# DeltaNet and a cosine-gated layer on one core: the key scales worked out in unused columns of a PSUM bank

## The chip, the cores and the metric

The kernel runs on one core of one Trainium2 chip. The metric is the time of one execution in microseconds on the device; the median of several executions is given. TensorE (PE in the profile, PEld its weight loads) multiplies matrices, VectorE (DVE) and ScalarE (ACT) work element by element, GpSimd (POOL) does so too, and SyncE (SP) issues most DMA transfers. SBUF is the working memory; PSUM takes the results of TensorE and can also be read and written by VectorE and ScalarE.

## The reference

Two layers, one after the other. Batch 4, 8 heads, 768 steps, head size 48:

```python
k_n = k / (np.linalg.norm(k, axis=-1, keepdims=True) + 1e-06)
for t in range(S):
    kt, vt, bt = (k_n[:, :, t], v[:, :, t], beta[:, :, t, None])
    y[:, :, t] = np.einsum('bhd,bhde->bhe', q[:, :, t], state)
    v_old = np.einsum('bhde,bhd->bhe', state, kt)
    state = state + bt[:, :, :, None] * np.einsum('bhd,bhe->bhde', kt, vt - v_old)
...
h = x @ w_in
g = h * np.cos(h)
return (g @ w_out).astype(np.float32)
```

Here x is y with its heads side by side: 3072 rows of 384. w_in has 2048 columns, and w_out leads back to 384. The norm of each key, with 1e-6 added, divides the key. The kernel keeps the keys as they are and moves the norm into two factors: beta / norm squared, which it multiplies into small tiles, and the norm itself, which it multiplies into the values v.

## The kernel before

The 768 steps are cut into 24 units of 32 steps. For each unit the kernel transposes keys and queries, forms the products of keys with keys and with queries (`gram`, L652), inverts a triangular matrix, and carries the state on: `through_state` (L907), `right_side` (L924), `solve` (L979), `solve_out` (L991), `update` (L1004), `update_out` (L1012, the state's addition on VectorE), `within` (L1034), `features` (L1055). Units 0 and 1 are inverted by doubling on TensorE (L736, L749 to L756), the others row by row on GpSimd (L856, L863; for units 2 and 3 partly on VectorE), with trips through DRAM. Units 2 and 3 have a further half step (`solve_half` L937, `between_out` L957, `solve` L973).

Every two units give 256 rows for the second layer, a "p". Its first products go to the three banks `p_h` (L1076 for the first two p, then L1250 by a scheme with fewer multiplications that needs sums of inputs and of weights); ScalarE and VectorE make g of them (L1113, L1120, L1129, L1132, with helpers L1262, L1264, L1267, L1348). The products with w_out go to the bank `p_out` (L1274 for the first p, then L1332 in seven products of 16 matmuls in the trace, written as two halves), from which ScalarE (L1371) and VectorE (L1384) collect them.

`p_out` is a tile of 2 x 256 fp32 columns, 2 KB for each partition. The products use 192 columns of either half in turn (`place`), `output` the first 384, and `keep_warm` (L492) writes the first 256 with products that nobody reads, until the first output begins; it fills TensorE in start-up. Columns 448 to 511 are used by nothing.

The scales of the keys come from a chain of small operations for each pair m of units: ScalarE squares the keys (L554), VectorE sums them over the head (L559), GpSimd raises the sum to the power 0.5 (L571, tile `knrm`), and then `scale` on VectorE adds 1e-6 (L582, in place), squares (L584), takes the reciprocal (L585), and forms `bs` = beta times it (L587) and `bz`, the same once for each of two kinds of row, masked by the constant `odd` (L590). For the first two pairs each unit has a call of its own with 8 columns; after them one call does both units with 16 columns. That makes 14 calls. `bs` and `bz` are read by `gram_keys` (L664, L673) and `solve_out`. `weigh` (L607) multiplies the values by the norm, in the later pairs after a copy that exchanges halves (L603, L605).

The order of all work is written out by hand: `Order.add` (L207) takes each task with its dependencies, and `Order.run` emits them in the sequence of the long string `LINE` (L101); every engine is then pinned to that order. So each engine executes its tasks in the written order, and an instruction that waits holds all behind it on its engine. The waits themselves are derived from which instructions read and write which tiles; they aren't written out in the kernel.

Of the kernel before, what the change touches and what calls it, by code (L numbers as in the profile page):

```python
# [10 lines left out]
FP = mybir.dt.float32  # L11
I32 = mybir.dt.int32
U32 = mybir.dt.uint32
ALU = mybir.AluOpType
# [225 lines left out]
def kernel(  # L240
# [32 lines left out]
    nc = tc.nc  # L273

    B, H, S, D = q.shape
# [17 lines left out]
    const = ctx.enter_context(tc.tile_pool(name="const", bufs=1))  # L293
# [3 lines left out]
    work = ctx.enter_context(tc.tile_pool(name="work", bufs=2))  # L297
# [27 lines left out]
    def half(i):  # L325
        return slice(DP * i, DP * i + DP)
# [105 lines left out]
    odd = consts[:, 128 + C : 130 + C]  # L432
# [9 lines left out]
    for b in range(B):  # L442
        nc.gpsimd.dma_start(
            out=bq[C * b : C * b + H].rearrange("p n t -> p (n t)"), in_=beta[b]
# [2 lines left out]

    halves = const.tile([128, 2, H], FP, name="halves")
    nc.vector.memset(halves, 0.5)
    tiny = const.tile([128, 2, H], FP, name="tiny")  # L450
    nc.vector.memset(tiny, 1e-6)
    halfpi = const.tile([128, 1], FP, name="halfpi")
    nc.vector.memset(halfpi, math.pi / 2.0)

# [9 lines left out]
    bt = const.tile([128, NU, H], FP, name="bt")  # L464
# [18 lines left out]

    HM = DM // 2
    p_out = psum.tile([128, 2, 256], FP, name="p_out", tag="o", bufs=1)


    out_begun = []
# [89 lines left out]
    def scale(m, part):  # L578

        n = part.stop - part.start  # L580
        bs, bz, knrm = (t[:, part] for t in scales[m])
        nc.vector.tensor_tensor(out=knrm, in0=knrm, in1=tiny[:, 0:n], op=ALU.add)  # L582
        krec = work.tile([128, 2, H], FP, name="krec")[:, 0:n]
        nc.vector.tensor_tensor(out=krec, in0=knrm, in1=knrm, op=ALU.mult)  # L584
        nc.vector.reciprocal(krec, krec)  # L585
        first = 2 * m + part.start
        nc.vector.tensor_tensor(  # L587
            out=bs, in0=bt[:, first : first + n], in1=krec, op=ALU.mult
        )
        nc.vector.tensor_tensor(  # L590
            out=bz,
            in0=bs[:, :, :, None].to_broadcast([128, n, H, 2]),
            in1=odd[:, None, None, :].to_broadcast([128, n, H, 2]),
            op=ALU.mult,
        )

    def weigh(m):

        vp, knrm = vps[m], scales[m][2]
        if 2 * m >= PLAIN_TURNS:  # L600

            t = work.tile([128, 2, H], FP, name="krec")
            nc.vector.tensor_copy(t[:, :, 0::2], knrm[:, :, 0::2])  # L603
            for i in range(2):
                nc.vector.tensor_copy(t[half(i), :, 1::2], knrm[half(1 - i), :, 1::2])  # L605
            knrm = t
        nc.vector.tensor_tensor(  # L607
            out=vp,
            in0=vp,
            in1=knrm[:, :, :, None].to_broadcast([128, 2, H, D]),  # L610
            op=ALU.mult,
        )

    def turn(n, tag):
# [346 lines left out]
    first, spare = {}, {}  # L961
# [431 lines left out]
    def store(p, i, cols=slice(0, DM)):  # L1393
# [7 lines left out]
        for b in range(B):  # L1401
# [9 lines left out]
            x=2, x_sum=XS, turns=2, g=GATES, o=2, o_out=2,  # L1411
# [59 lines left out]
    def unit(n):  # L1471
# [20 lines left out]
        if n < 4 or not second:  # L1492
            add(("square", m, a), "ACT", 0.2 + 0.37 * width, lambda: norms_square(m, part),
                [("k", 2 * m + x) for x in range(part.start, part.stop)],
                makes=[("g", ("ksq", m, a))])
            add(("sum", m, a), "DVE", 0.2 + 0.4 * width, lambda: norms_sum(m, part),
                [("square", m, a)], makes=[("ksum", ("ksum", m, a))], uses=[("ksq", m, a)])
            add(("norms", m, a), "POOL", 0.4 + 1.28 * width, lambda: norms_root(m, part),
                [("sum", m, a)] + ([("norms", m, 0)] if a else []),
                makes=[] if a else [("scales", ("scales", m))], uses=[("ksum", m, a)])  # L1500
            add(("scale", m, a), "DVE", 1.1, lambda: scale(m, part),
                [("norms", m, a), ("beta",) if n < PLAIN_TURNS else ("beta_home",)])
        scaled = ("scale", m, a if n < 4 else 0)
        if second:
            add(("weigh", m), "DVE", 1.1 if n < PLAIN_TURNS else 1.5, lambda: weigh(m),
                [("v", n - 1), ("v", n), ("scale", m, 0), scaled])
# [419 lines left out]
```

## Time and profile before

| what | value |
|---|---|
| time, median of 3 runs (lowest, highest) | 639.16 us (639.09, 640.67) |
| the profiled execution's own time | 643.63 us |
| its span, from the first to the last instruction | 641.8 us |
| TensorE busy up to 110 us, and from 110 to 642 us | 95.06 us, 525.93 us |
| VectorE busy in the same two stretches | 73.51 us, 422.26 us |
| granted TensorE clock in the same | 0.95, 1.00 |
| L582, VectorE, 14 instructions, start of the first and the last | 11.7 us, 451.4 us |

How to read it: a line such as `L582 DVE TENSOR_TENSOR knrm<-knrm,tiny` names the line of the kernel, the engine, the operation, and the tile written and those read. In the timeline the first number is the start in us from the span's start, the second the duration of the row, `x2` the number of instructions in it, and square brackets hold the idle time of that engine ahead of it and what ended it. A TensorE instruction on fp32 data shows as two rows in the trace, but for the transposes.

### The profile page before, as it was taken

Reading aid. Unit: us, or ns where it says so; the run is one execution under the profiler, and the core shown is the slowest. Engines: PE = TensorE matmul, PEld = TensorE weight load, DVE = VectorE, ACT = ScalarE, POOL = GpSimd, SP = SyncE. Lnnn points to the kernel's source line nnn. Section 1 sums busy time; section 2 is a strip of 40 time slices with the busy share of each in tenths; the row PEclk is TensorE's granted clock in tenths of the full one; section 3 lists DMA queues with packets and bytes.
Section 4 is the critical chain, followed back from the end, with each engine's and each line's share of the span. In section 5 each row is a group of like instructions: output and inputs, shape, how many; then the busy total and the mean of one; then the engine's idle time right before and its main releaser. Section 6 shows DMA issues by size and latency. Waiting matters only on the chain.

```text
span 641.8 us, 24181 instructions
## 1 busy us (share of the span) xinstructions
PE 621.0 (97%) x10176; PEld 577.7 (90%) x10176; DVE 495.8 (77%) x1025; ACT 297.6 (46%) x528; POOL 435.2 (68%) x780
## 2 busy tenths in 40 slices
PE   5999989999999999999999999999999999999997
PEld 4867877997899999999999999999999999999997
DVE  5786746788899999887888898888888786656682
ACT  3447645563334454643642544643643553545440
POOL 5337787778778788888789887886883883112231
PEclk9899989999999999999999999999999999999999
DMA  9869565563551454435436235243304102000000
GB/s 186 213 141 236 103 163 121 117 119 54 101 81 22 92 91 70 88 69 83 79 64 103 49 68 101 51 65 66 72 4 82 41 2 42 19 2 26 1 25 25
DMA packets 209380, 50.36 MB, mean 78 GB/s; under 512 B 200920, under 2 KB 204280, under 8 KB 209272
## 3 DMA queue, kind: packets, MB, share of 16 engines
q1 hardware_dynamic: 161896, 35.03, 29.2%
q10 hardware_dynamic: 47072, 13.25, 9.9%
q8 instruction: 80, 1.31, 0.8%
q0 software_dynamic: 304, 0.54, 0.4%
q14 instruction: 28, 0.23, 0.1%
HBM read 38.55 MB, written 10.22 MB: 76 GB/s over the span
## 4 chain that ended last, share of the span: by engine, by line
PE 88%; DVE 5%; DMA 3%; issue 1%; ACT 1%; SPq 0%; POOL 0%; ACTq 0%; DVEq 0%
PE p_out L1332 28%; PE p_h L1250 27%; PE p_h L1076 7%; PE p_kq L907 4%; PE p_out L1274 3%; PE p_s L1004 3%; PE p_g L652 3%; PE p_kq L1034 3%; PE p_u L979 2%; PE p_h L736 2%; PE p_out L492 2%; PE p_h L1332 2%; PE p_z L1055 1%; DMA kp<-in_k_dram 1%; DMA out_dram<-o 1%
## 5 line engine op out<-in xcount | busy, mean ns | idle before, releaser
L856 POOL TENSOR_TENSOR part<-z,gb 128x126 f32<-128x126 f32 (+23 forms) x321 | 142.5, 444 | 42.8 <-DMA gb<-g_dr 13.7
L863 POOL TENSOR_TENSOR z<-z,part 128x126 f32<-128x126 f32 (+23 forms) x321 | 146.0, 455 | 25.2
L1332 PE MATMUL p_out<-w_out,g_ffn 128*128 128x192 f32 x672 | 121.8, 328 | 1.3 <-ACT o L1371 0.7
L1332 PEld LDWEIGHTS p_out<-w_out,g_ffn 128*128 128x128 f32 x672 | 107.7, 190 | 2.5 <-ACT o L1371 0.8
L1129 ACT ACTIVATE turns<-turns,halfpi 128x512 f32<-128x512 f32 x96 | 68.0, 719 | 55.7 <-DVE turns L1120 43.0
L1332 PE MATMUL p_out<-w_sum,g_ffn 128*128 128x192 f32 x496 | 89.7, 329 | 0.2 <-DVE o L1384 0.2
L1250 PE MATMUL p_h<-x_sum,w_in 128*128 128x128 f32 x640 | 84.0, 277 | 0.0
L1332 PEld LDWEIGHTS p_out<-w_sum,g_ffn 128*128 128x128 f32 x496 | 79.6, 190 | 1.2 <-issue 0.4
L1113 ACT ACTIVATE turns<-g_ffn,quarter_turn 128x512 int32<-128x512 f32 x70 | 49.8, 719 | 66.1 <-DVE g_ffn L1267 23.5
L1250 PEld LDWEIGHTS p_h<-x_sum,w_in 128*128 128x128 f32 x640 | 78.8, 192 | 1.2
L1267 DVE TENSOR_TENSOR g_ffn<-g_ffn,p_h 128x512 f32<-128x512 f32 x80 | 54.2, 680 | 16.1 <-PE p_h L1250 15.4
L1120 DVE SCALAR_TENSOR_TENSOR turns<-g_ffn,turns 128x512 f32<-128x512 f32 x70 | 55.2, 795 | 13.2 <-ACT turns L1113 13.0
L1047 ACT COPY y<-p_kq 32x384 f32<-32x384 f32 x96 | 45.2, 470 | 34.1 <-PE p_kq L1034 25.3
L1132 DVE TENSOR_TENSOR g_ffn<-turns,g_ffn 128x512 f32<-128x512 f32 x70 | 51.9, 750 | 4.1 <-ACT turns L1129 4.0
L1250 PE MATMUL p_h<-x_sum,in_sum 128*128 128x128 f32 x400 | 53.0, 277 | 0.4 <-DVE g_ffn L1267 0.4
L571 POOL TENSOR_TENSOR knrm<-ksum,halves 128x16 f32<-128x16 f32 (+1 forms) x14 | 36.3, 2596 | 24.9 <-DVE ksum L559 24.9
L1250 PEld LDWEIGHTS p_h<-x_sum,in_sum 128*128 128x128 f32 x400 | 49.6, 192 | 1.5 <-DVE g_ffn L1267 0.7
L1384 DVE SCALAR_TENSOR_TENSOR o<-p_out,o 128x192 f32<-128x192 f32 x74 | 25.1, 351 | 29.5 <-PE p_out L1332 28.4
L1076 PE MATMUL p_h<-x_ffn,w_in 128*128 128x128 f32 x384 | 47.4, 283 | 0.0
L1076 PEld LDWEIGHTS p_h<-x_ffn,w_in 128*128 128x128 f32 x384 | 45.7, 198 | 1.2
L1250 PE MATMUL p_h<-x_ffn,w_in 128*128 128x128 f32 x320 | 42.4, 277 | 0.0
L1348 POOL TENSOR_TENSOR g_ffn<-g_ffn,g_ffn 128x512 f32<-128x512 f32 x18 | 25.8, 1442 | 23.1 <-PE p_out L1332 19.3
(163 smaller groups left out, 1072.1 us busy)
## 6 DMA issues: line engine op xcount, KB each, us to landing
g_ffn<-in_moe_w_in_dram SPq DMA_DIRECT2D x10, 512.0 KB
gb<-g_dr SPq DMA_DIRECT2D x14, 256.0 KB
vp<-in_v_dram SPq DMA_DIRECT2D x68, 48.0 KB
g_ffn<-in_moe_w_out_dram SPq DMA_DIRECT2D x8, 384.0 KB
g_ffn<-in_moe_w_out_dram ACTq DMA_DIRECT2D x8, 384.0 KB
kp<-in_k_dram SPq DMA_DIRECT2D x120, 24.0 KB
out_dram<-o SPq DMA_DIRECT2D x14, 192.0 KB
zt<-z_dr SPq DMA_DIRECT2D x72, 32.0 KB
```

Source lines behind the costliest of these rows:

```text
L571: nc.gpsimd.tensor_tensor(out=scales[m][2][:, part], in0=sums[m, part.start][:, 0:n], in1=halves[:, 0:n], op=ALU.pow,)
L856: eng.tensor_tensor(out=part, in0=z[:, 0:rows, j, None].to_broadcast(shape), in1=a[:, j, None, j + 1 :].to_broadcast(shape), op=ALU.mult,)
L863: eng.tensor_tensor(out=behind, in0=behind, in1=part, op=ALU.subtract)
L1047: nc.scalar.copy(by_parity(y[quarter(b)]), p_kq[quarter(b ^ 1), :, b % 2])
L1076: nc.tensor.matmul(p_h[:, i], w_in[:, t, (4 * k + i) * 128 : (4 * k + i + 1) * 128], xts[p][:, t, unit * 128 : (unit + 1) * 128], start=(i ...
L1113: nc.scalar.activation(turns[p, f], hidden_of(p, f), AF.Identity, bias=quarter_turn, scale=TURN)
L1120: nc.vector.scalar_tensor_tensor(out=r, in0=hidden_of(p, f), scalar=TURN, in1=t, op0=ALU.mult, op1=ALU.subtract,)
L1129: nc.scalar.activation(r, r, AF.Sin, bias=halfpi, scale=2.0 * math.pi)
L1132: nc.vector.tensor_tensor(out=place(p, f), in0=step_of(rests.pop((p, f)), f), in1=step_of(hidden_of(p, f), f), op=ALU.mult,)
L1250: nc.tensor.matmul(p_h[:, e], in_block(*w)[:, e], x_of(p, b), start=new and e == 0, stop=True, skip_group_check=True,)
L1267: nc.vector.tensor_tensor(out=part_of(p, to), in0=part_of(p, one), in1=part_of(p, two), op=op)
L1332: nc.tensor.matmul(p_o, left(p, part, a)[:, e % 4], right(e, b), start=(e == 0), stop=(e == FT // 2 - 1), skip_group_check=True,)
```

## The change

The tile `tiny` of 1e-6 goes. `scale` leaves `knrm` as it is. It adds 1e-6 with a constant (`tensor_scalar`) and writes the result into 8 or 16 of the 64 unused columns of `p_out` (`spare_out`; four calls take turns). It squares by an operation that reads `knrm` from SBUF and the first result from PSUM, takes the reciprocal in place, and forms `bs` from the PSUM columns and beta. `bz` is formed by two operations, one for each kind of row, that read the PSUM columns, beta, and one column of `odd` as a scalar for each partition, and no longer read `bs`. `weigh` adds the 1e-6 in the operation that multiplies the values.

```diff
-    tiny = const.tile([128, 2, H], FP, name="tiny")
-    nc.vector.memset(tiny, 1e-6)
...
     p_out = psum.tile([128, 2, 256], FP, name="p_out", tag="o", bufs=1)
+    spare_out = p_out[:, 1, HM:]
...
         bs, bz, knrm = (t[:, part] for t in scales[m])
-        nc.vector.tensor_tensor(out=knrm, in0=knrm, in1=tiny[:, 0:n], op=ALU.add)
-        krec = work.tile([128, 2, H], FP, name="krec")[:, 0:n]
-        nc.vector.tensor_tensor(out=krec, in0=knrm, in1=knrm, op=ALU.mult)
+
+        at = (2 * m + part.start) % 4 * 2 * H
+        krec = spare_out[:, at : at + n * H].rearrange("p (u h) -> p u h", h=H)
+        nc.vector.tensor_scalar(krec, knrm, 1e-6, None, op0=ALU.add)
+        nc.vector.scalar_tensor_tensor(
+            out=krec, in0=knrm, scalar=1e-6, in1=krec, op0=ALU.add, op1=ALU.mult
+        )
         nc.vector.reciprocal(krec, krec)
         first = 2 * m + part.start
-        nc.vector.tensor_tensor(
-            out=bs, in0=bt[:, first : first + n], in1=krec, op=ALU.mult
-        )
-        nc.vector.tensor_tensor(
-            out=bz,
-            in0=bs[:, :, :, None].to_broadcast([128, n, H, 2]),
-            in1=odd[:, None, None, :].to_broadcast([128, n, H, 2]),
-            op=ALU.mult,
-        )
+        beta_here = bt[:, first : first + n]
+        nc.vector.tensor_tensor(out=bs, in0=beta_here, in1=krec, op=ALU.mult)
+        for x in range(2):
+            nc.vector.scalar_tensor_tensor(
+                out=bz[:, :, :, x], in0=krec, scalar=odd[:, x : x + 1], in1=beta_here,
+                op0=ALU.mult, op1=ALU.mult,
+            )
...
-        nc.vector.tensor_tensor(
+        nc.vector.scalar_tensor_tensor(
             out=vp,
-            in0=vp,
-            in1=knrm[:, :, :, None].to_broadcast([128, 2, H, D]),
-            op=ALU.mult,
+            in0=knrm[:, :, :, None].to_broadcast([128, 2, H, D]),
+            scalar=1e-6,
+            in1=vp,
+            op0=ALU.add,
+            op1=ALU.mult,
         )
```

The order of the tasks is left as it was.

## The prediction

> **What bounds the kernel now.** I read the page first, then TensorE's waits in two windows, then the changed lines, then the timeline around each of their 14 places.
>
> ```profile
> PE 621.0 (97%) x10176; PEld 577.7 (90%) x10176; DVE 495.8 (77%) x1025; ACT 297.6 (46%) x528; POOL 435.2 (68%) x780
> ...
> PE p_out L1332 <- DVE o L1384: 0.8, 2, 0.6
> PE p_out L1332 <- ACT o L1371: 0.7, 1, 0.7
> PE p_h L1250 <- DVE g_ffn L1267: 0.4, 1, 0.4
> ```
>
> The first line is the page's: TensorE (PE) is busy 97% of the span. The other three are all its waits from 110 us to the end: 0.8 + 0.7 + 0.4 = 1.9 us in 532 us. So behind 110 us TensorE sets the time. VectorE (DVE, 77%) gains nothing there by being quicker, while whatever makes TensorE wait is added to the end nearly whole. Ahead of 110 us TensorE has idle time that a quicker VectorE may close: 1.21 us ahead of L736 at 38.06, and 2.07 us at 83.70 ahead of the last matmuls of L973, for which the view names no releaser ("issue").
>
> What the change is aimed at is in the view of line 582:
>
> ```profile
> L582 DVE TENSOR_TENSOR knrm<-knrm,tiny x14: 121/168/1250, 11.7 to 451.4; 128x16 f32<-128x16 f32 x10, 128x8 f32<-128x8 f32 x4
> ```
>
> Minimum, median and maximum are 121, 168 and 1250 ns for 8 or 16 elements. The longest stand beside POOL's additions. Busy time of the five lines 582, 584, 585, 587 and 590 is 4.8 + 4.0 + 3.3 + 2.8 + 3.1 = 18.0 us. At their medians (168 + 175 + 253 + 174 + 191 = 961 ns with 16 elements, about 870 with 8) 14 scales would take 10 x 0.96 + 4 x 0.87 = 13.1. So 4.9 us is stretching, of which 2.1 lies in one scale at 33.27 and 1.07 in the first instruction at 366.15. [...]
>
> **One scale, old and new.** Old, undisturbed: 961 ns and four steps of 34 ns between dependent instructions, 1.10 us; with 8 columns 1.02 (11.65 to 12.67). The trace has no VectorE write to PSUM, so I take the fixed part of nearby rows that read it. L673 (256 elements, 414 ns) and L991 (384, 547) give 1.04 ns an element and 148 fixed. L1384 (scalar_tensor_tensor, 192, 356) has 156 fixed, L924 (the same with a per-partition scalar, 409) has 209, and L775 (SBUF tensor_scalar, 128, 280) has 147. With 16 elements (17 ns): add 164, square 173, reciprocal 253, bs 165, and two bz of 226 each, which need no wait and start some 80 ns before their forerunner ends (as L924's pairs do). The sum is 164 + 34 + 173 + 34 + 253 + 34 + 165 + 2 x (226 - 80) = 1.15 us; with 8 columns 1.06. ScalarE writes 512 columns to PSUM in 570 ns (L1262 to p_h) and to SBUF in 586, so a PSUM output need not be dear. Bounds: 1.0 (the old one less 0.1) to 1.5 (six instructions with 60 ns more each, about what L924 has over L1384). [...]
>
> The lost memset of tiny (72 ns at the start) is nothing. In weigh, 12 instructions turn from tensor_tensor to scalar_tensor_tensor with the same two SBUF inputs: medians of 684 (L1132) and 693 (L1120) for 512 elements, 12 x 14 ns off the path, nothing. DMAs and all engines' orders stay as they were.
>
> **The new waits.** The built kernels' instruction lists side by side show what the diff doesn't: p_out is one PSUM bank, which TensorE writes all the time, and the unused columns are ordered with all else in that bank. The first instruction of a scale now waits for the last TensorE write (and ScalarE read) of p_out ahead of it in the written order; the next matmul into p_out waits for the scale's last instruction. [...] Ordered by columns the waits would fall away and the sum be about -1.1 us, start-up alone; by the bank it is that below.
>
> Ten matmuls into p_out and one ScalarE copy get such a wait. I set the old end of each scale beside the old start of its waiter. With room (end, start): 15.90 and 18.07, 58.03 and 64.38, 226.18 and 226.75, 272.30 and 274.25, 426.15 and 427.09, 452.72 and 453.68. These cost nothing; what hides them is TensorE's own other matmuls, and the smallest cover is 0.57 us. Without room are five places.
>
> (a) At 199.96 the product must wait for a scale that begins at 200.59, behind the state's addition:
>
> ```profile
> 199.72 0.94 DVE L1012 TENSOR_TENSOR st<-st,p_s 128x768 f32<-128x768 f32 x1
> ...
> 199.96 1.57 PE L1332 MATMUL p_out<-w_sum,g_ffn 128*128 128x192 f32 x8
> ...
> 200.59 0.16 DVE L582 TENSOR_TENSOR knrm<-knrm,tiny 128x16 f32<-128x16 f32 x1
> ```
>
> TensorE resumes at 200.59 + 1.15 + 0.06 = 201.80: **+1.84**. Queued behind are L1250's and L907's matmuls, all later.
>
> (b) At 327.57 the scale waits in mid-product:
>
> ```profile
> 327.57 0.17 DVE L582 TENSOR_TENSOR knrm<-knrm,tiny 128x16 f32<-128x16 f32 x1
> ...
> 328.55 2.87 PE L1332 MATMUL p_out<-w_out,g_ffn 128*128 128x192 f32 x16 [0.68 <-ACT o L1371]
> ...
> 328.78 0.95 DVE L1012 TENSOR_TENSOR st<-st,p_s 128x768 f32<-128x768 f32 x1
> ...
> 331.51 0.36 DVE L1384 SCALAR_TENSOR_TENSOR o<-p_out,o 128x192 f32<-128x192 f32 x1 [0.59 <-issue]
> ```
>
> It is written between the product's two halves. The first half's last matmul ends at 330.12, so VectorE idles for 2.6 us with L1012, L1348 and L1267 behind it; the scale runs 330.17 to 331.32, and the second half, which began at 329.96, begins at 331.37: **+1.41**. VectorE is late by 2.46, of which its idle 0.59 and TensorE's own lag take all but about 0.4. I count that as nothing, and up to 1.0 in the range.
>
> (c) At 366.15 the scale waits for a product that ends at 368.75:
>
> ```profile
> 366.15 1.24 DVE L582 TENSOR_TENSOR knrm<-knrm,tiny 128x16 f32<-128x16 f32 x1
> ...
> 367.28 1.47 PE L1332 MATMUL p_out<-w_out,g_ffn 128*128 128x192 f32 x8
> ...
> 368.43 0.74 DVE L924 SCALAR_TENSOR_TENSOR rhs<-p_kq,consts,vp 128x192 f32<-128x192 f32 x2
> ...
> 370.46 0.68 PE L979 MATMUL p_u<-rhs,zt 64*64 64x48 f32 x32
> ```
>
> It ends at 368.80 + 1.15 = 369.95 instead of 368.52, stretching and all. L924's rhs is ready at 371.27 for 369.82; TensorE's L979 had 0.64 of room, so +0.85, and the next meeting (L991's u at 373.62, L1004 at 373.95, room 0.33) makes it **+1.1**.
>
> (d) At 82.09 a filling matmul (L492) must wait for a scale that ends at 84.47, 2.4 us. Behind it stands L973, which idles for 2.07 us at 83.70 anyway. If what that idle time waits for comes at its own time, the wait fits in: **+0.1**; if it moves along, +2.4. The page has 80 loads on an instruction queue; one of them could be the cause, and its request would then be older than the wait. I take the low end.
>
> (e) Start-up: at 33.27 and 36.34 two scales come one behind the other, and 2.1 us of stretching goes. They would end at 35.31, not 37.34. But the filling matmul of 34.73 now waits for them, until 35.36, +0.63, then TensorE reaches L736 at 37.48, whose input is ready: 0.58 before its old 38.06. With 0.04 more for each of the scales at 11.65 and 14.93, which stand in the opening chain: **-0.5**. Bounds: -1.2 (the whole idle time) to +0.6.
>
> **Sum:** 1.84 + 1.41 + 1.1 + 0.1 - 0.5 = 3.95 us on the profiled execution (span 641.8, its time 643.63). That one is 4.5 us above the median of the runs, so I carry the microseconds over: 639.16 + 3.95 = **643.1 us**, 0.6% slower. About 0.3% (1.9 us) is what a measurement of this kernel tells from no change.
>
> **Rivals.**
>
> 1. *Faster: the stretching was on the path.* In start-up TensorE's 1.21 us at 38.06 goes whole, and at 366.15 the 1.07 us count too, while the waits fall where TensorE has run ahead. 639.16 - 1.2 - 1.07 = 636.9. For it: VectorE's line 756 releases L736 at 38.06. Against it: the four waits in (a) to (c) are in the written order, and TensorE had no idle time beside (a) and (c). It decides if the matmul after a scale comes over 1.2 us behind its start. Chance 0.08.
> 2. *Absorbed.* The others run ahead while TensorE stands, its 1.9 us of waits behind 110 us vanish, and start-up gives all of 1.2: 643.1 - 1.9 - 0.7 = 640.5. Against it: those waits are on work that TensorE itself released. Chance 0.14.
> 3. *The stalls spread.* (d) costs its 2.3 more, VectorE's lag of (b) 1.0, and (c) 0.3: 646.7. Chance 0.14.
> 4. *PSUM is dear*, 0.35 us more per scale: three times in (a) to (c), twice in the opening chain: 643.1 + 1.75 = 644.9. Chance 0.08.
> 5. [...] Chance 0.01.
>
> The forecast, 641.6 to 645, has the other 0.55. The range of 640.0 to 646.9 leaves out rival 1, some of 2 and what lies above 3, less than 0.2. Slower by over 0.3%: 0.55 + 0.14 + 0.08 + a quarter of rival 2 = 0.81; faster 0.08; within 0.3% the remaining 0.11.
>
> **What would show it.** New idle time of TensorE ahead of the products' matmuls of 1.8 and 1.4 us, near 200 and 330; VectorE idle 2.6 us ahead of a scale's first instruction near 327 and 366; L979 late near 370; the idle 2.07 at 83.70 shrunk or gone, with L492 waiting in its stead; scale instructions of 150 to 260 ns with no outlier over 400. The forecast is wrong if TensorE's idle time behind 110 us stays near 1.9 us, or if scales take 1.5 us.

## The result and the profile after

The changed kernel takes 645.76 us (median of 11 runs, 642.86 to 649.03). The kernel before, beside it on the same chip, takes 639.71 us (11 runs, 639.09 to 644.39). The ratio is 1.0083, with a 95% interval of 1.0059 to 1.0107: slower by 0.8%, that is by 5.3 us on 639.7 (3.8 to 6.8 by the interval). The forecast was +3.95 us, 643.1, in a range of 640.0 to 646.9.

The profiled execution of the changed kernel took 646.31 us with a span of 644.5. First the busy line of its page, then TensorE's waits from 110 us to the end (us in total, times, longest), as the prediction showed them for the kernel before. Line numbers behind the scale have grown by 3: L1335 is the product into `p_out`, L584 to L593 is the scale, L491 the filling matmul.

```profile
PE 623.1 (97%) x10176; PEld 579.3 (90%) x10176; DVE 488.8 (76%) x1038; ACT 297.6 (46%) x528; POOL 435.7 (68%) x780
```

```profile
PE p_out L1335 <- DVE bz L593: 3.0, 2, 1.6
PE p_u L982 <- PE p_h L1253: 0.5, 1, 0.5
PE p_g L655 <- issue: 0.3, 1, 0.3
PE p_out L1335 <- DVE o L1387: 0.2, 1, 0.2
PE p_out L1335 <- ACT o L1374: 0.2, 1, 0.2
PE p_s L1007 <- DVE u L994: 0.2, 1, 0.2
```

VectorE is busy 488.8 us where it was 495.8, with 13 more instructions. The operations have become cheaper, as the change intends: TensorE's waits have grown all the same. The first row is new and is the scale's last operation (L593) holding up a product twice, for 1.6 and 1.4 us. The other waits together are 1.4 us where the kernel before had 1.9.

Here is place (a), in TensorE's and in VectorE's timeline (start, duration, engine, line; in brackets the idle time before it and what ended it):

```profile
199.33 0.88 PE L1037 MATMUL p_kq<-u,tt 32*32 32x48 f32 x64
201.83 1.41 PE L1335 MATMUL p_out<-w_sum,g_ffn 128*128 128x192 f32 x7 [1.62 <-DVE bz L593]
```

```profile
199.74 0.94 DVE L1015 TENSOR_TENSOR st<-st,p_s 128x768 f32<-128x768 f32 x1
200.60 0.16 DVE L584 TENSOR_SCALAR p_out<-knrm 128x16 f32<-128x16 f32 x1
...
201.40 0.37 DVE L593 SCALAR_TENSOR_TENSOR bz<-p_out,consts,bt 128x16 f32<-128x16 f32 x2
```

The scale is one operation behind the state's addition (L1015) and runs from 200.60 to 201.77, 1.17 us. The product starts 0.06 after it. Both were forecast: 1.15 us, and a start at 201.80. Places (b) and (c), on VectorE:

```profile
330.87 0.18 DVE L584 TENSOR_SCALAR p_out<-knrm 128x16 f32<-128x16 f32 x1 [2.09 <-POOL z L866]
...
370.37 0.18 DVE L584 TENSOR_SCALAR p_out<-knrm 128x16 f32<-128x16 f32 x1 [2.60 <-PE p_out L1335]
...
371.47 0.73 DVE L927 SCALAR_TENSOR_TENSOR rhs<-p_kq,consts,vp 128x192 f32<-128x192 f32 x2
```

VectorE stands still 2.09 and 2.60 us, since its next operation in order may not write the bank before TensorE's half of the product is done (at 330.87 the view names POOL, one of whose additions happens to end at 330.74, while the product's eighth matmul ends at 330.73; at 370.37 it names the product). Behind it stands L927, whose rhs TensorE's L982 needs: 0.51 us of idle time at 372.12 (the view names TensorE's own L1253, whose row ends at that moment). At (b) the second half of the product waits 1.38 us.

And place (d), TensorE's timeline from 80 us:

```profile
80.03 0.88 PE L940 MATMUL p_v<-g_ffn,in_sum 32*32 32x48 f32 x64
83.28 1.22 PE L491 MATMUL p_out<-o 128*128 128x256 f32 x2 [2.37 <-DVE bz L593]
84.43 1.50 PE L976 MATMUL p_u<-g_ffn,w_sum 32*32 32x48 f32 x64
85.86 4.87 PE L1079 MATMUL p_h<-x_ffn,w_in 128*128 128x128 f32 x24
```

The filling matmul waits 2.37 us, L976 then passes all its 64 matmuls without the idle time that the kernel before had at its 59th, and so far this is the forecast. What was not in it is the duration of the rows behind the wait. Two filling matmuls take 1.22 us instead of 0.70, and 24 matmuls of L1079 take 4.87 us instead of the 2.94 that another execution of the kernel before shows below. The granted clock tells why. In the table of stretches the row is: stretch, its length, busy time and count of each engine, granted TensorE clock, DMA share and GB/s.

```profile
78.00:80.90 2.90, 2.88 (x136) 2.16 (x134) 0.00 (x0) 1.48 (x3) 2.90 (x4) 1.00 0.97 233
83.20:86.00 2.80, 2.72 (x67) 1.96 (x67) 0.03 (x1) 1.18 (x3) 2.25 (x8) 0.50 0.51 150
86.00:88.00 2.00, 2.00 (x10) 2.00 (x11) 1.88 (x4) 1.56 (x4) 1.69 (x5) 0.50 0.43 73
88.00:90.00 2.00, 2.00 (x11) 2.00 (x11) 0.00 (x0) 0.34 (x1) 1.61 (x5) 0.52 0.70 190
90.00:92.00 2.00, 2.00 (x41) 1.54 (x39) 0.30 (x1) 0.00 (x0) 1.69 (x4) 1.00 0.19 18
```

Behind the wait TensorE is granted half its clock, from 83.09 to 89.92 us. It is busy all the time, so no list of waits shows this loss.

### The profile page after: what moved, and what is told of

It reads as the page before. It is cut to its first block, busy times and chain, and to the rows that moved or that the text cites. A ratio compares the mean times of both kernels' runs of the same rounds, so it can differ in the third digit from the quotient of the medians.

```text
span 644.5 us, 24204 instructions
## 1 busy us (share of the span) xinstructions
PE 623.1 (97%) x10176; PEld 579.3 (90%) x10176; DVE 488.8 (76%) x1038; ACT 297.6 (46%) x528; POOL 435.7 (68%) x780
## 4 chain that ended last, share of the span: by engine, by line
PE 85%; DVE 5%; POOL 3%; DMA 3%; issue 2%; ACT 1%; ACTq 1%; SPq 0%; DVEq 0%; POOLq 0%
PE p_out L1335 27%; PE p_h L1253 25%; PE p_h L1079 7%; PE p_kq L910 4%; PE p_out L1277 3%; PE p_g L655 3%; PE p_h L739 3%; PE p_s L1007 3%; PE p_out L491 2%; PE p_kq L1037 2%; PE p_u L982 2%; PE p_h L1335 2%; POOL part L859 1%; PE p_z L1058 1%; POOL z L866 1%
## 5 line engine op out<-in xcount | busy, mean ns | idle before, releaser
L1335 PE MATMUL p_out<-w_out,g_ffn 128*128 128x192 f32 x672 | 122.1, 328 | 1.5 <-DVE bz L593 1.4
L1335 PEld LDWEIGHTS p_out<-w_out,g_ffn 128*128 128x128 f32 x672 | 107.7, 190 | 3.0 <-DVE bz L593 1.7
L1335 PE MATMUL p_out<-w_sum,g_ffn 128*128 128x192 f32 x496 | 89.8, 329 | 1.8 <-DVE bz L593 1.6
L1253 PE MATMUL p_h<-x_sum,w_in 128*128 128x128 f32 x640 | 84.0, 277 | 0.0
L1335 PEld LDWEIGHTS p_out<-w_sum,g_ffn 128*128 128x128 f32 x496 | 79.6, 190 | 3.0 <-DVE bz L593 1.8
L1253 PEld LDWEIGHTS p_h<-x_sum,w_in 128*128 128x128 f32 x640 | 78.8, 192 | 1.1
L1135 DVE TENSOR_TENSOR g_ffn<-turns,g_ffn 128x512 f32<-128x512 f32 x70 | 50.5, 731 | 4.2 <-ACT turns L1132 4.0
L570 POOL TENSOR_TENSOR knrm<-ksum,halves 128x16 f32<-128x16 f32 (+1 forms) x14 | 36.8, 2627 | 24.3 <-DVE ksum L558 23.7
L1253 PE MATMUL p_h<-x_sum,in_sum 128*128 128x128 f32 x400 | 52.9, 277 | 0.0
L1253 PEld LDWEIGHTS p_h<-x_sum,in_sum 128*128 128x128 f32 x400 | 49.7, 192 | 0.8
L1079 PE MATMUL p_h<-x_ffn,w_in 128*128 128x128 f32 x384 | 47.7, 284 | 0.0
L1079 PEld LDWEIGHTS p_h<-x_ffn,w_in 128*128 128x128 f32 x384 | 46.0, 199 | 1.2
L1253 PE MATMUL p_h<-x_ffn,w_in 128*128 128x128 f32 x320 | 42.4, 277 | 0.0
```

The source lines that it names most:

```text
L570: nc.gpsimd.tensor_tensor(out=scales[m][2][:, part], in0=sums[m, part.start][:, 0:n], in1=halves[:, 0:n], op=ALU.pow,)
L1079: nc.tensor.matmul(p_h[:, i], w_in[:, t, (4 * k + i) * 128 : (4 * k + i + 1) * 128], xts[p][:, t, unit * 128 : (unit + 1) * 128], start=(i ...
L1135: nc.vector.tensor_tensor(out=place(p, f), in0=step_of(rests.pop((p, f)), f), in1=step_of(hidden_of(p, f), f), op=ALU.mult,)
L1253: nc.tensor.matmul(p_h[:, e], in_block(*w)[:, e], x_of(p, b), start=new and e == 0, stop=True, skip_group_check=True,)
L1335: nc.tensor.matmul(p_o, left(p, part, a)[:, e % 4], right(e, b), start=(e == 0), stop=(e == FT // 2 - 1), skip_group_check=True,)
```

## The experiments

Two theories stood against each other at first. **Bank:** the new operations cost what the old ones did, and the whole loss is the order that the shared bank imposes. **Price:** the six operations on PSUM are dear. Behind the profile a third question came up: what the half clock costs, and when it comes. In the diffs a line of "..." leaves out what is unchanged.

**The kernel before, once more.** No edit. The profiled execution that the prediction rests on lay 3.9 us above the median of its kernel, and its idle time at 83.70 was the reason for costing (d) at nothing.

> The kernel before, unchanged, profiled a second time. The profiled execution of before took 643.63 us, 3.9 above the median of its eleven runs (639.71); that of the changed kernel 646.31, only 0.5 above its median (645.76). So the two profiles differ by 2.7 us and the medians by 6.0. Theory A: the 2.07 us of TensorE's idle time at 83.70 in the first profile of before (releaser not named) is no property of the kernel but of that execution; a second profile shows it gone or much shorter and takes about 641 us or less. Theory B: the idle time comes again at the same matmuls of L973 (1.5 us or more), and the 3.3 us that the profiles don't explain lie elsewhere.

Measured: 640.15 us, span 638.3, mean granted clock 0.997. The idle time came again at the same matmul, as theory B has it, but shorter, followed by full clock, and in the time of theory A. TensorE's timeline of this execution, and a stretch of it with the clock:

```profile
82.94 0.86 PE L973 MATMUL p_u<-g_ffn,w_sum 32*32 32x48 f32 x59
85.32 0.28 PE L973 MATMUL p_u<-g_ffn,w_sum 32*32 32x48 f32 x5 [1.52 <-issue]
85.53 2.94 PE L1076 MATMUL p_h<-x_ffn,w_in 128*128 128x128 f32 x24
```

```profile
87.00:89.00 2.00, 2.00 (x42) 1.88 (x44) 0.53 (x1) 1.75 (x4) 1.62 (x5) 1.00 0.67 193
```

And the same of the execution in the prediction:

```profile
85.77 0.28 PE L973 MATMUL p_u<-g_ffn,w_sum 32*32 32x48 f32 x5 [2.07 <-issue]
85.98 4.57 PE L1076 MATMUL p_h<-x_ffn,w_in 128*128 128x128 f32 x24
```

```profile
88.00:89.50 1.50, 1.50 (x9) 1.50 (x9) 0.00 (x0) 1.24 (x3) 1.20 (x4) 0.50 0.69 208
```

The same 24 matmuls take 2.94 us behind 1.52 us of idle time and 4.57 us behind 2.07. So the execution that I predicted from already had a stretch of half clock in it, 3.41 us long, and I read its rows without the clock beside them.

**The intermediate in SBUF.** All new operations, with no shared bank:

```diff
-        krec = spare_out[:, at : at + n * H].rearrange("p (u h) -> p u h", h=H)
+        krec = work.tile([128, 2, H], FP, name="krec")[:, 0:n]
```

> The changed kernel with the intermediate krec in an SBUF tile instead of the spare columns of p_out; all instructions else as changed. Theory 'bank waits': no wait on p_out is left, so the time falls back to that of before, 639.7 us within 1.5; the scales are stretched beside POOL again. Rival 'the new operations are dear': six instructions with per-partition scalars instead of five cost the same here, so the time stays at 645 or more.

Measured: 641.60 us (12 runs) beside 640.77 (23 runs of the kernel before), ratio 1.0002 (0.9987 to 1.0017). Without the PSUM columns the loss is gone, so it isn't the six operations in place of five. The bank's waits and a price of PSUM would both go with the columns; the next two kernels tell them apart. This kernel also shows what the PSUM columns buy, in the view of the scale's first line (minimum, median, maximum in ns):

```profile
L584 DVE TENSOR_SCALAR krec<-knrm x14: 129/190/1253, 11.2 to 449.4; 128x16 f32<-128x16 f32 x10, 128x8 f32<-128x8 f32 x4
```

And of the changed kernel:

```profile
L584 DVE TENSOR_SCALAR p_out<-knrm x14: 148/170/179, 11.4 to 454.4; 128x16 f32<-128x16 f32 x10, 128x8 f32<-128x8 f32 x4
```

With its output in PSUM none of the 14 is stretched, though POOL works beside 12 of them; with its output in SBUF it still is (1253 ns), though it reads one SBUF input only. So an operation with one SBUF input was stretched beside POOL too. Undisturbed it costs the same on either side: the shortest with 16 columns take 158 ns with the output in SBUF and 159 in PSUM.

**The waits alone.** The kernel before, with one spare column of `p_out` set ahead of each scale and copied away behind it:

```diff
+    spare_out = p_out[:, 1, HM:]
+    touched_out = const.tile([128, 1], FP, name="touched_out")
...
+        touch = spare_out[:, at : at + 1]
+        nc.vector.memset(touch, 0.0)
         nc.vector.tensor_tensor(out=knrm, in0=knrm, in1=tiny[:, 0:n], op=ALU.add)
...
+        nc.vector.tensor_copy(touched_out, touch)
```

> The kernel before with its own five operations on SBUF, and beside them one memset of a single spare column of p_out ahead of each scale and one copy of that column to SBUF behind it: the waits of the change without its operations. Theory 'bank waits': 644 to 649 us, as the changed kernel or up to 2 us above it, since each scale is two small instructions (about 0.25 us) longer and the stretching beside POOL stays. Rival 'the new operations are dear': about 640, two small instructions in 14 places that lie beside TensorE.

Measured: 649.33 us (4 runs), ratio 1.0126 (1.0106 to 1.0145). TensorE's waits from 30 us on begin with:

```profile
PE p_out L494 <- DVE touched_out L601: 5.1, 2, 2.6
PE p_out L1338 <- DVE touched_out L601: 3.3, 2, 1.8
```

The waits come at the same places as in the changed kernel, and at 34 us besides, where the old, stretched scales take longer. They make the kernel slow without any of the new operations, a little above the 644 to 649 us expected: "bank" stands.

**All waits moved away.** The changed kernel, with four edits of the written order, so that each scale of (a) to (c) stands at a point where the bank is free, and the filling matmul of (d) ahead of its scale:

```diff
+            (('scale', 5, 0), 1, ('collect', 1, 4)),
+            (('scale', 8, 0), 0, ('layer_out', 5, 16)),
+            (('scale', 9, 0), 1, ('collect', 5, 1)),
+            (('warm', 29), 0, ('scale', 3, 0)),
+        ):
+            line.remove(key)
+            line.insert(line.index(at) + after, key)
```

> The changed kernel with four tasks moved in the written order, so that no matmul into p_out stands behind a scale that is still to run: the filling matmul of 82.09 ahead of the scale, the scale of 200.6 to right behind the collection at 198.3, that of 327.6 ahead of the ScalarE copy of 328.2, that of 366.2 behind that of 368.8. Theory 'bank waits': the 1.6, 1.4 and 0.8 us of idle time go and the wait at 82 too, and the gain in start-up stays: 638 to 640.5 us. Rival 'the new operations are dear', or other places cost: 643 or more.

Measured: 641.26 us (12 runs), ratio 1.0000 (0.9987 to 1.0013). The four places hold the whole loss, and the six operations on PSUM, which are all still there, cost nothing that this ratio shows: "price" has fallen. But the time is above the 638 to 640.5 us expected. In the profile TensorE is ahead of the second execution of the kernel before, by 1.7 us at 38 us and still by 1.4 at 200, and later waits, most of them on VectorE and ScalarE, give it back.

**Only (d) moved.** The last of the four edits alone.

> The changed kernel with one edit in the written order: the filling matmul of place (d) stands ahead of the scale of the third turn, so that it has nothing to wait for; the waits of (a), (b) and (c) stay. In the changed kernel this wait was 2.37 us, TensorE ran its matmuls at half clock for the 6.8 us behind it, and it lost 3.4 us there against the kernel before whose idle time at this place was 1.5 us. Theory clock (what the idle time triggers is dear, not the idle time itself): the idle time here goes back to about 1.5 us ahead of the small matmuls of L976, no half clock follows, and the kernel is about 3 us below the changed one: some 642.5, ratio to the kernel before 1.003 to 1.006. Rival, the forecast's own reason (the wait lies in an idle time that comes anyway, so it costs 0.1): taking it away gives 0.1 to 0.9 us, about 645, ratio 1.007 to 1.008.

Measured: 645.33 us (6 runs), ratio 1.0072 (1.0045 to 1.0098), 0.0011 below the changed kernel. My theory of the moment missed by 3 us, and the rival's number came out. But the rival's reason didn't: in the profile the idle time is back at 1.55 us and half clock follows it this time. It also follows the 1.69 us of (a), where the changed kernel ran on at full clock behind 1.62 us (1.00 from 201.9 to 203.2 us). A stretch behind (a) with only (d) moved:

```profile
199.90:201.50 1.60, 1.60 (x7) 1.60 (x6) 0.06 (x1) 0.06 (x1) 1.36 (x4) 0.50 0.00 0
```

So a length above which half clock comes, such as the 1.8 us that I had in mind, isn't the rule. Where each stretch of half clock begins tells more: within one execution the beginnings and ends lie on one grid of 3.413 us (for this kernel at 15.53, 83.79 and 199.85: 20 and 54 times 3.413 us after the first), whose phase differs from execution to execution. Laid over TensorE's idle time, window by window, in all fourteen profiles from 25 to 630 us, this grid gives: all six full-clock windows with 1.80 us of idle time or more are followed by half clock, none of those with less than 1.41 is, and of the ten from 1.41 to 1.75 four are (1.43, 1.59, 1.59 and 1.69). By these windows it counts whether 1.4 to 1.8 us of the 3.41 are idle, and so also where the window begins; a sharp bound doesn't come out of them. (Some windows at half clock were followed by a second one, as in the changed kernel at 83.09, without much idle time in them; why isn't settled.) An idle time of 1.4 to 2.1 us is a lottery, and the kernel before draws in it too, at its 83.70.

**The first two pairs of units ("turns" in the expectations) alone in PSUM.** An attempt at a better version:

```diff
+        if m < 2:
             krec = spare_out[:, at : at + n * H].rearrange("p (u h) -> p u h", h=H)
+        else:
+            krec = work.tile([128, 2, H], FP, name="krec")[:, 0:n]
```

> The changed kernel with its intermediate in the spare PSUM columns for the first two turns alone (four scales) and in an SBUF tile of the work pool from the third turn on. By the reading of the traces, what the change brought at the start (TensorE's 1.21 us of idle time at 38 us gone) stays, and the waits of (a) to (d) go with the shared bank: about 1 us below the kernel before if that gain is kept to the end, ratio 0.998 to 0.999. Rival, absorbed: the gain at the start is given back at later meetings, as in the kernel with all four waits moved away, and the ratio is 0.9995 to 1.0005.

Measured: 639.17 us (12 runs) beside 640.47 (23), ratio 0.9987 (0.9968 to 1.0006), and in a second series:

> The version with the spare PSUM columns for the first two turns alone once more, since its first interval (0.9968 to 1.0006) left open whether it beats the kernel before. If the start-up gain is real and mostly kept, ratio 0.997 to 0.9995 again, and both series together lie below 1; if the first was chance, ratio 0.9995 to 1.001.

Measured: 639.50 us (12 runs) beside 640.50 (17), ratio 0.9980 (0.9965 to 0.9995). This one beats the kernel before by about 1 us, as far as the second interval tells. That this is the start-up gain, kept in part, isn't shown: the spans of its two profiles are 637.2 and 639.3 us, on either side of the 638.3 of the second execution of the kernel before.

**A short and a long wait.** The kernel before, with the bank's wait at place (a) only. The copy that ends the wait stands behind the reciprocal in the short one:

```diff
+        if m == 5:
+            nc.vector.memset(touch, 0.0)
...
         nc.vector.reciprocal(krec, krec)
+        if m == 5:
+            nc.vector.tensor_copy(touched_out, touch)
...
+        if m == 5:
+            for _ in range(2):
+                nc.vector.memset(padding, 0.0)
```

In the long one the same copy stands at the very end, behind the padding; the instructions are the same.

> The kernel before, with the waits of the shared bank at one place alone, the scale of the sixth turn near 200 us: a column of the output bank is set ahead of this scale and copied away behind its reciprocal, so that the product's next matmul waits for four small operations; two small operations of padding stand behind it. Both theories: TensorE stands idle there for about 1.3 to 1.5 us and runs on at full clock; TensorE is later by that much, and the kernel some 1.0 to 1.5 us slower where later work does not take it up, ratio 1.001 to 1.0025.

> The same instructions as in the short one, but the copy that closes the wait stands behind the two operations of padding: the wait is about 0.7 us longer, 2.0 to 2.2 us. Theory clock (idle time from about 1.8 us on is followed by half clock for 3.4 us or more): the granted clock behind the gap is 0.5, and TensorE's later matmuls are 0.7 plus 1.5 to 2.0 us later than in the short one, so the ratio rises by about 0.0035. Rival, length alone counts: full clock behind the gap, 0.7 us later, ratio higher by 0.001.

Measured: 641.50 us (12 runs), ratio 1.0014 (0.9999 to 1.0030), for the short one; 646.02 (6 runs), ratio 1.0075 (1.0047 to 1.0102), for the long one. Stretches behind the wait, short and then long:

```profile
199.90:201.40 1.50, 1.50 (x10) 1.50 (x11) 1.38 (x5) 1.04 (x3) 1.27 (x4) 1.00 0.00 0
201.40:203.00 1.60, 1.60 (x17) 1.60 (x16) 0.57 (x2) 0.00 (x0) 1.32 (x4) 1.00 0.00 0
```

```profile
202.70:203.60 0.90, 0.90 (x5) 0.90 (x6) 0.58 (x1) 0.06 (x1) 0.74 (x3) 1.00 0.00 0
203.70:205.00 1.30, 1.30 (x7) 1.30 (x6) 0.00 (x0) 0.00 (x0) 1.06 (x4) 0.50 0.00 0
205.00:207.00 2.00, 2.00 (x11) 2.00 (x11) 0.45 (x1) 0.00 (x0) 1.61 (x6) 0.50 0.00 0
207.20:209.00 1.80, 1.80 (x72) 1.60 (x70) 1.48 (x4) 1.25 (x3) 1.52 (x4) 1.00 0.00 0
```

The wait is 1.47 us in the short one and 2.46 in the long one. Behind the long wait TensorE starts at full clock, falls to half at 203.65, when the window ends, and stays there for 3.41 us. Matched matmul by matmul, the long one loses 0.94 us by its longer wait and a further 1.81 by 212 us, close to half of 3.41. So 2.75 us of the 4.5 between the medians are shown at this place. The rest isn't settled: in the profiles it lies near 85 us (2.65), where the long one's execution drew half clock and the short one's didn't. Length alone would have given 1.0. The clocks of all the runs agree: their mean is 0.995 in the short one and 0.992 in the long one, which by the measure given below is 1.2 windows of half clock more.

**The idle time at the 59th matmul.** The page has 80 loads of 16 KB on an instruction queue, and TensorE has 20552 instructions in the trace (20352 matmuls and weight loads, and 200 others), 257 for each. To see whether the idle time at L973 waits for such a load, the five first filling matmuls are cut, so that 70 more stand ahead of it:

```diff
     for _ in range(Order.WARM_FIRST):
-        keep_warm()
+        for c in range(0, 256, 32):
+            nc.tensor.matmul(
+                p_out[:, 0, c : c + 32], out_tiles[0][:, 0:128], out_tiles[0][:, 128 + c : 160 + c]
+            )
```

> The kernel before, with its five first filling matmuls of 256 columns each cut into eight of 32 columns: 70 more matmuls in the trace, as many columns. Theory load (TensorE's 1.5 to 2.1 us of idle time near 82 us, put down to issue, waits for a 16 KB load of its next instructions, of which the trace has 80, for 20552 matmuls and weight loads, so one for 128 matmuls with their loads; it comes there because 128 matmuls of 14 ns each pass faster than a load): 70 more matmuls ahead of it move the end of the block to 70 matmuls earlier, among others, and the idle time at the 59th matmul of L973 is gone; TensorE is up to 1.5 us earlier behind 90 us, half clock no longer follows there, and the time is 1.5 to 2.5 us below the kernel before, ratio 0.996 to 0.998, with no more than 1 us of idle time put down to issue at any place. Rival (the idle time belongs to that matmul or its operands): it stays at the 59th matmul of L973, 1.5 to 2.1 us, ratio 0.999 to 1.001.

> The version with the spare PSUM columns for the first two turns alone, and with the first filling matmuls cut as in the other run of this call. Theory load: both gains add up, no idle time of TensorE over 1 us behind 25 us, no half clock behind 25 us, 3 to 4 us below the kernel before, ratio 0.994 to 0.9955. Rival: as without the cut, ratio 0.9985 to 0.9995.

Measured: 652.46 us (5 runs), ratio 1.0186 (1.0159 to 1.0212), and 652.32 (6 runs), ratio 1.0183 (1.0155 to 1.0211). The times missed altogether: a filling matmul of 32 columns takes 0.22 us at the start, where one of 256 takes 0.46, so that eight for one make start-up 12 us longer. Of the place, half came out: the idle time has left the 59th matmul of L973, but stands elsewhere, where none over 1 us was expected. TensorE's timeline of the first of the two:

```profile
93.66 0.88 PE L976 MATMUL p_u<-g_ffn,w_sum 32*32 32x48 f32 x64
...
99.61 0.81 PE L655 MATMUL p_g<-kq_t 48*32 48x64 f32 x59
101.85 0.31 PE L655 MATMUL p_g<-kq_t 48*32 48x64 f32 x5 [1.43 <-issue]
```

L976 passes its 64 matmuls without a gap. The idle time now stands in L655. In the trace's count it came behind 1479 matmuls before and comes behind 1735 now, 2 x 128 more: the ends of blocks of 128 matmuls, fixed in the count and not in the code. In this execution a 16 KB load lies at 99.43 to 100.31 us, and at 82.53 to 83.88 in the second execution of the kernel before. TensorE goes on 1.54 and 1.44 us after the load's end. In the execution of the prediction it is 1.46 (84.31 and 85.77). So the idle time goes with a load that has its own due time. TensorE gains 1.7 us at L973 against the second execution of the kernel before and loses 1.6 at L655, and more behind it at half clock. A shift that gives the gain without that loss wasn't tried.

**(b) and (c) alone.** The first and the last of the four moves.

> The changed kernel with the waits of (a) and (d) taken away by the written order, those of (b) and (c) left. Theory (the waits' idle time adds up, and half clock comes on top only where a stretch of 3.4 us has about 1.6 us or more of idle time in it, which the 1.4 us of (b) don't reach): (b) and (c) cost 1.4 and 1.3 us, less 0.5 to 0.9 taken up, ratio 1.003 to 1.0045, and the mean granted clock of the runs is that of the kernel before. Rival (the whole excess over the forecast lies in (b) and (c)): ratio 1.006 or more.

Measured: 643.14 us (12 runs), ratio 1.0044 (1.0028 to 1.0060). The first of TensorE's waits from 110 us on are 1.4 us at (b) and 0.5 at (c):

```profile
PE p_out L1341 <- DVE bz L599: 1.4, 1, 1.4
PE p_u L988 <- PE p_h L1259: 0.5, 1, 0.5
```

The mean granted clock of its runs is 0.995, as in the kernel before (0.995 over the runs beside the experiments). The changed kernel's is 0.992. A window of half clock takes 3.41 x 0.5 = 1.7 us from a span of 640, 0.0027 of the mean. So the changed kernel has about 3.0 such windows in each run, and the kernel before 1.9; some of them lie ahead of 25 us, where TensorE waits for others anyway. With only (d) moved the mean is 0.992 as well, 3.0 windows, and with (a) moved too 1.8. So by the clocks the added windows come with the wait of (a).

## Why the prediction was right, and which terms were mis-sized

The direction and the mechanism held. The bank orders the scale with everything else in `p_out`, the cost lies in the five places named, the operations are 1.17 us and none over 270 ns, and PSUM's price lay within its bounds. The sum came out at 5.3 us for 3.95, which is still within the measured interval of 3.8 to 6.8; that it came so near is in part luck, since by the trace several terms were off, up and down. In the table, "by trace" is TensorE's delay against the second execution of the kernel before, matched matmul by matmul; "by ratio" is the difference of two kernels' ratios times 640 us. A ratio is known to about 0.0013 to 0.0026, so the last column is good to 1 to 2.3 us; it adds up to 5.3 by the way it is made.

| term | forecast | by trace | by ratio |
|---|---|---|---|
| (a) | +1.84 | +1.82 | +1.8 (only (d) moved, less (b) and (c) alone) |
| (b) and (c) | +1.41, +1.1 | +1.8, +1.27 | +2.8 |
| (d) | +0.1 | +3.4 | +0.7 (changed, less only (d) moved) |
| (e) start-up | -0.5 | -1.3 | 0.0 (all four moved) |
| between the places | none | +0.25 - 0.9 | |

**(a), (b) and (c)** are right in mechanism, and in size as far as the waits themselves go. In (b) VectorE's lag, which I costed at nothing, adds 0.27.

**(d)** failed in its reason's second half. The wait did fit into the idle time: the load that L973 waits for comes at its own time, which the cut filling matmuls show. But I priced an idle time by its length. 2.37 us in the place of 1.52 is 0.85, and two windows at half clock make it 3.4 in this execution. By the ratios it is less, 0.7, which they don't tell from 0.1. Half clock comes here without the wait too: of the ten profiles in which this idle time comes by itself (1.50 to 2.07 us), three go on at half clock, the one that I started from among them; both with the wait do (2.37 us, and 2.5 with the waits alone).

**(e)** looks larger in the profile than it is. TensorE is 1.3 us ahead at 38 us, but part of that is an operation ahead of the first scale that the change doesn't touch. VectorE's timeline of the kernel before, and then of the changed one:

```profile
31.87 1.48 DVE L533 TENSOR_SCALAR w_in<-w_in 128x512 uint32<-128x512 uint32 x1
```

```profile
31.93 0.42 DVE L532 TENSOR_SCALAR w_in<-w_in 128x512 uint32<-128x512 uint32 x1
```

It took 0.93 us in the second execution of the kernel before. Over the profiles with an uncut start it takes 0.38 to 0.42 us in some and 0.92 to 1.48 in others, with old scales and with new. In two profiles with the old scales at this place and the short operation (the short and the long wait) TensorE reaches this matmul at 37.0 us; in four with the scales in PSUM and the short operation it does at 36.0 to 36.8. That is a gain of 0.2 to 1.0 us, for 0.5 forecast. And the kernel with all four waits moved away is no faster than before: what TensorE is ahead it gives back to VectorE and ScalarE later, which is rival 2's mechanism, on the start-up gain. Whether the moved scales bring some of those later waits themselves wasn't tested. That the scales' stretching would go was part of this term, and nothing in the profile before showed it; in the changed kernel it is gone (no operation of a scale over 267 ns, where the kernel before has 1250), and with the intermediate in SBUF it is still there (1253).

**The half clock** appears in no term. 1.1 more windows in each run, at 1.7 us, is an estimate of 1.9 us from the mean clocks, if these windows lie where TensorE sets the time, which a mean doesn't show. It lies within the rows of the table and not beside them. By the clocks the wait of (a) draws these windows, though in the one profile of the changed kernel it didn't; that of 1.4 us in (b) adds none. How the 1.35 us above the forecast divide between the terms stays open, since the last column is no finer than that.

Of the rivals, 3 (646.7) and 4 (644.9) both came within 1 us of the measured time, and both were wrong in kind. With rival 3, (d)'s loss isn't the idle time moving along. Rival 4's dear operations are refuted by the scale's 1.17 us and by the version with all waits moved, whose scales stand in PSUM; the same version refutes rival 1's stretching on the path, since it has neither stretching nor waits and is no faster.

## What to carry to other kernels

The unused columns of this PSUM bank weren't free storage while TensorE was writing the bank: in the built kernel every access stood in order with all the others, and these waits alone, without the new operations, took the kernel before to a ratio of 1.0126. So look for the nearest neighbours of each access in the written order before placing one there. Price TensorE's idle time by more than its length: from about 1.4 us on it cost some 1.7 us more here for each window at half clock (1.81 by the trace behind the wait of 2.46 us), in some executions and not in others, so read the granted clock beside any stretch from which you take a duration. And take such durations from more than one execution, since one of them may already hold what you are trying to predict.

## What the runs showed of the hardware

- Half clock came in windows of 3.41 us on a grid fixed within an execution. Of the full-clock windows it followed all six with 1.80 us of idle time or more, four of the ten with 1.41 to 1.75, and none with less. It lowers the mean granted clock by 0.0027 for each window here (0.992 in the first profile of the kernel before, with three of them), so the mean clock of a run counts them.
- TensorE stood idle for 1.4 to 2.1 us, put down to "issue", among small matmuls of 14 ns each, and in three executions went on 1.44 to 1.54 us after the end of a 16 KB load on an instruction queue. The trace has 80 such loads, by an estimate from its 20552 instructions one for 128 matmuls with their weight loads; 70 more matmuls ahead moved the place by 2 x 128 in the count. That these matmuls outrun the loads of their instructions is my reading; no run shows it by itself.
- A VectorE operation of 16 columns that adds a constant cost the same with its output in PSUM as in SBUF (159 and 158 ns at least), and with its output in PSUM it wasn't stretched beside GpSimd (at most 179 ns over the 14, with 8 or 16 columns, against 1253).
